# One other hand-written order, in which VectorE makes two early products and GpSimd takes half of e from the first unit on

## The chip, the cores and the metric

The kernel runs on one core of a Trainium2 chip. The time is the device time of one execution in microseconds (us); lower is better. Five instruction streams matter here, each strictly in order: TensorE (PE), VectorE (DVE), ScalarE (ACT), GpSimd (POOL) and SyncE (SP), which only issues DMAs. An execution has a span (first to last instruction in the profile) and a time of its own that is a little longer than the span.

## What is computed

Two layers are fused: a gated recurrence along the sequence, and a highway feed-forward layer on its result. With x and f_logit of shape (4, 6336, 256):

```python
sig = 1.0 / (1.0 + np.exp(-f_logit))
f = lower_bound + (1.0 - lower_bound) * sig        # per channel
for t in range(S):
    h = f[:, t] * h + (1.0 - f[:, t]) * x[:, t]
    y[:, t] = h
H = np.maximum(y @ w_h, 0.0)                       # tokens flattened
T = 1.0 / (1.0 + np.exp(-(y @ w_t + b_t)))
out = T * H + (1.0 - T) * y
```

All inputs and the output are float32 in HBM: 52 MB are read and 26 MB written.

## The kernel before, in words

**Tiles.** Work is cut into 25 units. Units 0 to 23 hold 1024 tokens of one batch entry as 8 blocks of 128 tokens, and unit n continues the recurrence of unit n-4. Unit 24 holds the last 192 tokens of all four batch entries as 8 blocks of 96. The recurrence half of a unit is called a *front*, the feed-forward half a *back*. `CUTS` (L44) cuts some units: unit 0 has three fronts (2, 2 and 4 blocks), units 1 and 2 have two fronts of 4 blocks, and unit 24 has two fronts and two backs of 4 blocks. So there are 30 fronts and 26 backs: fronts 0, 1 and 2 are unit 0, fronts 3 and 4 are unit 1, fronts 5 and 6 are unit 2, and front n is unit n-4 for n from 7 to 27. Back j is unit j up to 23; backs 24 and 25 are the halves of unit 24.

**Steps of a front.** Each step has a letter in the order described below. The channels lie in two halves h of 128.

- L, X (L106, SP): the DMA of f_logit into `lt` and of x into `xt`; 1 MB for a whole unit.
- U (L158, ACT): u = sigmoid(-lt), for all 8 blocks in one instruction.
- P (L164, POOL) or p (L170, DVE): bv = u * xt, two blocks to an instruction, so four for a whole unit. Which products are p and not P stands in the list `EARLY` (L69), which is empty here.
- A (L202, PE): 8 transposes of u into PSUM (uT); F (L209, ACT): f = 1 + ncc*uT, one instruction for each h.
- B (L219, PE): 4 transposes of bv into PSUM (bT); S (L234, DVE): the scan y = f*y + bT, one for each h.

**Steps of a back.** W (L152, DVE) makes the weights `w_sb` once, from w_h and w_t, which Q (L129, SP) loads. G and Z (L249, PE) are the matmuls gp and zp, four of 512 columns for each h; both read the y of both channel halves. T (L255, ACT): t = sigmoid(zp + b_t). D (L260, DVE): d = max(gp, ncc*y). E (L170, DVE) and H (L164, POOL): e = d*t, E the first columns and H the rest. O (L300, L301, PE): the output tokens of 4 blocks in PSUM, from y and e. C (L307, ACT) and V (L307, DVE) copy them to SBUF; V does a share in the last three backs only. R (L313, SP) stores them.

**Who does e.** `shared` (L265) gives the number of columns of e that GpSimd makes: 512 of 1024 for full backs from back 3 on, none for backs 0 to 2, whose e DVE makes in one instruction of 128x2048.

**The port rule.** `gpsimd_mul` (L162) makes each GpSimd product wait for every DVE product (E or p) that stands before it in the order since the last GpSimd product.

**The order.** It is written out by hand: `PLAN` (L353) is a string in which each letter issues the next instance of its step, and every engine executes its instructions in the order of the string. In A, B, Z, G and O the digit behind the letter is the PSUM slot. uT and bT share two small slots, gp, zp and op share three large ones, and a step waits until the one before in its slot has been read. M (L373, PE) is a matmul on a tile of zeros whose result nobody reads; 22 of them lie in the first part of the string. L and X wait for a free buffer of five each (`BUFS`, L78), and SP issues loads and stores from one queue, so that a store that waits for its copy holds back the loads behind it.

In the running part both engines that matter most go round like this, once for a unit: DVE `S D E S D`, ACT `F T C F T C U` in changing order. D works on the unit whose scan was finished just before.

Of the kernel before, what the change touches and what calls it, by code (L numbers as in the profile page):

```python
# [19 lines left out]
def kernel(  # L20
# [19 lines left out]
    P = 128  # L40
    NH = D // P
    NB = 8
# [16 lines left out]
    fronts, backs = [], []  # L59
# [6 lines left out]

    LASTQ = 2

    EARLY = []  # L69

# [40 lines left out]
    def shape(piece):  # L113

        u, j0, j1 = piece
        return units[u][0], j1 - j0
# [38 lines left out]
    def gate(i):  # L155
        np_, nb = shape(fronts[i])
        u = fs[i]["u"] = new("u", [NB, D], FP16)
        pin(nc.scalar.activation(u[:np_, :nb], fs[i]["lt"][:np_, :nb], AF.Sigmoid, scale=-1.0))  # L158
# [13 lines left out]
    def product(i, k, mul):  # L172
        np_, _ = shape(fronts[i])
        if "bv" not in fs[i]:
            fs[i]["bv"] = new("bv", [NB // 2, D, 2], BF16)
        mul(inner(fs[i]["bv"][:np_, k:k + 1])[:, 0], fs[i]["u"][:np_, 2 * k:2 * k + 2],
            fs[i]["xt"][:np_, 2 * k:2 * k + 2])

    def width(piece):
        np_, nb = shape(piece)  # L180
        return np_ * nb
# [81 lines left out]
    SHARE = 512  # L263

    def shared(j):  # L265

        return SHARE if width(backs[j]) == NB * P and j >= 3 else 0

    def e_cols(j, a, e):
        if "e" not in bs[j]:  # L270
# [3 lines left out]
    def e_dve(j):  # L274
        vector_mul(*e_cols(j, 0, width(backs[j]) - shared(j)))

    def e_pool(j):
        gpsimd_mul(*e_cols(j, width(backs[j]) - shared(j), width(backs[j])))
# [37 lines left out]
    def each(pieces, count):  # L316
        return [(i, k) for i, piece in enumerate(pieces) for k in range(count(piece))]

    def halves_of(pieces):
        return each(pieces, lambda p: len(halves(p)))  # L320
# [11 lines left out]
        "U": (lambda i, _: gate(i), each(fronts, lambda p: 1)),  # L332
        "P": (lambda i, k: product(i, k, gpsimd_mul), [p for p in products if p not in EARLY]),
        "p": (lambda i, k: product(i, k, vector_mul), [p for p in products if p in EARLY]),
        "A": (decay_pe, halves_of(fronts)),
# [7 lines left out]
        "D": (d_dve, each(backs, lambda p: NH)),  # L343
        "E": (lambda j, _: e_dve(j), each(backs, lambda p: 1)),
        "H": (lambda j, _: e_pool(j), [(j, 0) for j in range(len(backs)) if shared(j)]),
        "O": (o_pe, groups),
        "C": (lambda j, q: o_copy(j, q, nc.scalar.copy, 0, group(j, q)[2]), [p for p in groups if group(*p)[2]]),
# [3 lines left out]
    }  # L351

    PLAN = (  # L353
        "XLLLXXLXLQQUUMMMMMMMMMMMA0MA1PFFFUFUMB0PSSMMMMB1A0FFPSSPMMMMMB1A0XLLXLXXPFUFSSWWPB1A0G0Z1PFFUPSSDPXL"
        "LXLB0A1G2Z0PUTFFTPPB1SSDUSSEZ1A0G0G2A1DDPFTFFPPZ1A0B1O0O2PSSTFECCUB0Z1B1G0G2SDSDA0Z0TUFTPPPPPPA0G1B1"
        "FXLLLXRRXLXDESA0Z0Z2O1UFTCTB0G0A1O1O2SDPPPFCCB1A0Z1G0O2FTUCB0G1PPPHPSDSEDPA1Z0Z2B0O1FTUCTESA1G0G1B0D"
        "DHPPPPSZ2O0O1FUTCCB1SA0G2Z0B1FDUTPHPPSXXLRLRRRLRXLRRZ1A0G2O0PDTFCEEG1B1A0O2O0UFCCDSG1B0A1Z2Z0SDPHPPP"
        "PFTTA1B0O2O1G0HPSFCCZ2B1A0Z1DUTFTEG0O2PSPLXXRXRRRRDPPHCB1SA0O1G0Z2B1FCUTDEPSG1Z0A0O2FTCPDPPHB1A0Z1G0"
        "O2SFTCDEB0Z1A1G0PLLXRRRRSDPPPUFTO2B0A1Z0G1SHDCFTEO2B0G0Z1A1PPPPCUFTSDHO2B0A1G0Z1SCFTO2B0A1DEPSZ1G0PP"
        "PCUFTDHO2B0A1O0G1SCFCDEZ2B0A1Z0PSTFTPPPG1B1O2A0O0DUCFCSG1Z2A1B0HDELXLLRXRLLRXRRRRRXPSTFPPZ1G0O2B1DTC"  # L360
        "SZ1G2A0O0PHUFTCDEB1A0G2Z1O0PSPFTCDPPHB0G1G2A1Z0UFTSA0B1FDEDSPO1O0Z2B0PPCCTPHSO1A1G0Z2B0UFTCDEPSA1G0Z"
        "2O1PPDB0FTCSA1Z2G0O1PHFUCTDELXRRXXRRLRLXXRRRA1B0G0Z1PSFTO2DCB1A0G1Z0O2PPPHSUFCTDEB1A0Z1G2O0PSDFTCB0A"
        "1Z1G2SFPPPHDO0B1A0G2ETUCFPSO1PZ0CDTB1A0Z1G2SFTUHO0A0B1DFG1EPPPPSO2A0CCZ0DFB1O2Z1B0TCUTSESHPPG0A1Z2G1"
        "DDRRRRRRRRFFTA1B0O2Z0Z1FCFSEHTTG2B1G0O1RSDDCO2SRHCZ0G1STRO2TDDEZ0CTERTG1O2O0DVDVCO2CREVO1CRO0RCVRR"
    )
    assert set(PLAN) <= {*kinds, *"M012"}
    assert all(PLAN.count(k) == len(places) for k, (_, places) in kinds.items())
# [36 lines left out]
```

## Time and profile before

| what | value |
|---|---|
| median of 3 runs | 212.41 us (211.95 to 212.56) |
| profiled execution, its own time | 212.41 us |
| its span | 210.6 us |
| DVE busy | 195.0 us (93%) |
| ACT busy | 193.6 us (92%) |
| PE busy | 191.6 us (91%), mean granted clock 0.989 |
| POOL busy | 160.7 us (76%) |
| DMA | 78.69 MB, 374 GB/s over the span |

An engine's busy time is the union of its instructions' spans. On ACT one instruction's span can reach into the next one's, so the distance from start to start is the better measure of what an instruction costs there. "Idle before" in the groups is the time that the engine had nothing under way, with the instruction or the transfer that ended it.

### The profile page before, as it was taken

How to read it: one execution, taken by the hardware profiler on the slowest of the kernel's cores; microseconds unless marked ns; L12 is line 12 of the kernel's file. 1: busy time of each engine (PE TensorE's matmuls, PEld its weight loads, DVE VectorE, ACT ScalarE, POOL GpSimd, SP SyncE). 2: the span in 40 equal slices, each digit the busy share in tenths (PEclk: the TensorE clock that was granted, in tenths of full speed). 3: DMA queues.
4: the chain of work that ended last, by engine and by line, in shares of the span. 5: the costliest groups of instructions: out<-in, count | busy, mean ns of one | idle time of the engine just before them, and what ended most of it. 6: DMA issues, size and time to landing. Idle time of an engine off the chain costs nothing.

```text
span 210.6 us, 4661 instructions
## 1 busy us (share of the span) xinstructions
PE 191.6 (91%) x1822; PEld 132.3 (63%) x1822; DVE 195.0 (93%) x155; ACT 193.6 (92%) x194; POOL 160.7 (76%) x133
## 2 busy tenths in 40 slices
PE   7759988899889999999999999999999999999970
PEld 2336564586565866767667666658576676855770
DVE  2379999999999999999999999999999999999980
ACT  3687999999999999999999999999999999998750
POOL 4667685797799698978998898898889867866400
PEclk9997999999999999999999999999999999999998
DMA  5999999999999999999999999999999997252465
GB/s 133 416 409 429 422 429 428 428 422 419 422 426 422 416 424 419 429 426 415 425 419 429 426 420 426 423 413 429 417 428 412 365 412 310 100 204 100 195 261 195
DMA packets 17350, 78.69 MB, mean 374 GB/s; under 512 B 2352, under 2 KB 2864, under 8 KB 11952
## 3 DMA queue, kind: packets, MB, share of 16 engines
q1 hardware_dynamic: 16784, 78.39, 90.9%
q8 instruction: 14, 0.23, 0.4%
q10 hardware_dynamic: 544, 0.00, 0.1%
q14 instruction: 8, 0.07, 0.1%
HBM read 52.43 MB, written 25.95 MB: 372 GB/s over the span
## 4 chain that ended last, share of the span: by engine, by line
ACT 45%; PE 35%; issue 10%; DMA 3%; POOL 1%; DVE 1%; SPq 1%; ACTq 1%; POOLq 0%; DVEq 0%
ACT t L255 15%; ACT f L209 11%; ACT u L158 10%; PE zp L249 10%; ACT o L307 9%; PE gp L249 7%; PE op L300 5%; PE op L301 5%; PE uT L202 4%; PE bT L219 4%; DMA xt<-in_x_dram 3%; POOL bv L164 1%; SPq L106 1%; DVE o L307 1%; DVE y L234 1%
## 5 line engine op out<-in xcount | busy, mean ns | idle before, releaser
L164 POOL TENSOR_TENSOR bv<-u,xt 128x512 bf16<-128x512 f16 (+1 forms) x100 | 114.4, 1175 | 29.9 <-DVE e L170 13.4
L234 DVE TENSOR_TENSOR_SCAN y<-f,y,bT 128x1024 bf16<-128x1024 f16 (+3 forms) x56 | 106.4, 1917 | 2.3 <-PE bT L219 2.1
L209 ACT ACTIVATE f<-uT,ncc 128x1024 f16<-128x1024 f16 (+3 forms) x60 | 65.3, 1104 | 2.0 <-PE uT L202 2.0
L255 ACT ACTIVATE t<-zp,bt 128x1024 bf16<-128x1024 f32 (+1 forms) x52 | 63.1, 1238 | 0.3 <-DVE e L170 0.3
L260 DVE SCALAR_TENSOR_TENSOR d<-y,ncc,gp 128x1024 bf16<-128x1024 bf16 (+1 forms) x52 | 62.4, 1209 | 0.3 <-issue 0.2
L249 PEld LDWEIGHTS <-w_sb 128*128 128x128 f16 x400 | 37.8, 98 | 37.4 <-issue 5.6
L307 ACT COPY o<-op 128x1024 f32<-128x1024 f32 (+2 forms) x50 | 54.7, 1142 | 4.1 <-PE op L301 2.1
L158 ACT ACTIVATE u<-lt 128x2048 f16<-128x2048 f32 (+3 forms) x30 | 53.1, 1774 | 4.2 <-DMA lt<-in_f_logit_dram 4.2
L249 PE MATMUL gp<-y,w_sb 128*128 128x512 bf16 (+1 forms) x200 | 51.0, 380 | 0.8 <-ACT o L307 0.2
L249 PE MATMUL zp<-y,w_sb 128*128 128x512 bf16 (+1 forms) x200 | 50.4, 376 | 1.2 <-DVE d L260 0.6
L300 PE MATMUL op<-diag,y 128*128 128x128 f16 (+1 forms) x400 | 49.2, 219 | 1.9 <-ACT t L255 0.7
L164 POOL TENSOR_TENSOR e<-d,t 128x1024 bf16<-128x1024 bf16 x21 | 44.8, 2133 | 7.5 <-DVE e L170 2.6
L301 PE MATMUL op<-ident_b,e 128*128 128x128 bf16 (+1 forms) x400 | 49.2, 219 | 0.0
L301 PEld LDWEIGHTS <-e 128*128 128x128 bf16 (+1 forms) x400 | 44.7, 114 | 5.6 <-issue 3.4
L300 PEld LDWEIGHTS <-y 128*128 128x128 bf16 (+1 forms) x400 | 44.8, 114 | 2.7
L219 PE MATMUL bT<-ident_f,bv 128*128 128x128 f32 (+1 forms) x200 | 31.6, 279 | 4.1 <-DVE y L234 1.6
L202 PE MATMUL uT<-ident_h,u 128*128 128x128 f16 (+1 forms) x400 | 30.9, 220 | 4.0 <-ACT f L209 2.3
L202 PEld LDWEIGHTS <-u 128*128 128x128 f16 (+1 forms) x400 | 26.4, 99 | 11.3 <-issue 5.3
L219 PEld LDWEIGHTS bT<-ident_f,bv 128*128 128x128 f32 (+1 forms) x200 | 22.5, 143 | 11.2 <-POOL bv L164 5.0
L170 DVE TENSOR_TENSOR e<-d,t 128x1024 bf16<-128x1024 bf16 (+2 forms) x26 | 19.1, 741 | 0.1
L234 DVE TENSOR_TENSOR_SCAN y<-f,bT 128x512 bf16<-128x512 f16 (+2 forms) x8 | 10.5, 1339 | 2.8 <-PE bT L219 2.8
L373 PE MATMUL busy<-filler 128*128 128x512 bf16 x22 | 7.2, 468 | 1.2 <-DVE filler L120 1.2
(22 smaller groups left out, 12.8 us busy)
## 6 DMA issues: line engine op xcount, KB each, us to landing
out_dram<-o SPq DMA_DIRECT2D x48, 512.0 KB, 13.5
lt<-in_f_logit_dram SPq DMA_DIRECT2D x21, 1024.0 KB, 14.9
xt<-in_x_dram SPq DMA_DIRECT2D x21, 1024.0 KB, 15.9
lt<-in_f_logit_dram SPq DMA_DIRECT2D x5, 512.0 KB, 7.6
xt<-in_x_dram SPq DMA_DIRECT2D x5, 512.0 KB, 8.2
lt<-in_f_logit_dram SPq DMA_DIRECT2D x2, 384.0 KB, 13.0
xt<-in_x_dram SPq DMA_DIRECT2D x2, 384.0 KB, 11.6
xt<-in_x_dram SPq DMA_DIRECT2D x2, 256.0 KB, 4.5
```

Source lines behind the costliest of these rows:

```text
L158: pin(nc.scalar.activation(u[:np_, :nb], fs[i]["lt"][:np_, :nb], AF.Sigmoid, scale=-1.0))
L164: ins = pin(nc.gpsimd.tensor_mul(out_, a, b))
L202: pin(nc.tensor.transpose(uT[:, j * np_:(j + 1) * np_], fs[i]["u"][:np_, j, h * P:(h + 1) * P], ident_h[:np_, :np_]))
L209: pin(nc.scalar.activation(f[:, :N].rearrange("p (k q j) -> p k q j", q=np_, j=j), fs[i]["uT", h].rearrange("p (k j q) -> p k q j", q=np_, ...
L219: pin(nc.tensor.transpose(t[:, k // r, k % r], fs[i]["bv"][:np_, k, h * P:(h + 1) * P].rearrange("p d j -> p (d j)").bitcast(FP32), ident_ ...
L234: pin(nc.vector.tensor_tensor_scan(y, fs[i]["f", h][:, c:c + w], fs[i]["bT", h][:, c:c + w], 0.0 if prev is None else prev, op0=ALU.mult, ...
L249: pin(nc.tensor.matmul(p[:, a:e], w_sb[:, k, ki, h * P:(h + 1) * P], y_of(j)[:, ki, a:e], start=ki == 0, stop=ki == NH - 1))
L255: pin(nc.scalar.activation(bs[j]["t"][:, m, :width(backs[j])], bs[j]["zp", m], AF.Sigmoid, bias=bt[:, m:m + 1]))
L260: pin(nc.vector.scalar_tensor_tensor(bs[j]["d"][:, m, :width(backs[j])], y_of(j)[:, m], ncc[:, m:m + 1], bs[j]["gp", m], op0=ALU.mult, op1 ...
L300: pin(nc.tensor.matmul(o, y[:, h, cols], diag[:, h], start=True, stop=False))
L301: pin(nc.tensor.matmul(o, bs[j]["e"][:, h, cols], ident_b, start=False, stop=True))
L307: pin(copy(bs[j]["o", q][:np_, a:e], bs[j]["op", q][:np_, a:e]))
```

## The change

`EARLY` names two products: the one of front 0 and the first of front 2 are made on DVE (letter p). `shared` no longer asks for j >= 3, so that GpSimd makes half of e for backs 0 to 2 as well (three more H; E of these backs shrinks to 128x1024). And the whole string `PLAN` is another one. Its letters are the same but for the two p in place of two P, three more H, and 21 M in place of 22. The order differs nearly everywhere: the first loads are L0 L1 X0 X1 L2 X2 and then the weights, S of front 3 stands behind G, G, Z and D, D of back 0, stores stand further ahead among the loads, and the last steps of back 25 (Z, T, T, E) stand further back.

```diff
-    EARLY = []
+    EARLY = [(0, 0), (2, 0)]
...
     def shared(j):
 
-        return SHARE if width(backs[j]) == NB * P and j >= 3 else 0
+        return SHARE if width(backs[j]) == NB * P else 0
...
     PLAN = (
-        "XLLLXXLXLQQUUMMMMMMMMMMMA0MA1PFFFUFUMB0PSSMMMMB1A0FFPSSPMMMMMB1A0XLLXLXXPFUFSSWWPB1A0G0Z1PFFUPSSDPXL"
-        "LXLB0A1G2Z0PUTFFTPPB1SSDUSSEZ1A0G0G2A1DDPFTFFPPZ1A0B1O0O2PSSTFECCUB0Z1B1G0G2SDSDA0Z0TUFTPPPPPPA0G1B1"
+        "LLXXLXQQUUMMMMMMMMMA0pFFMMMMB1PSLXLXLXLSA0MMMMB1UFFpSSWWMMA0PFFUXLXLMMB1PSA0PSUFFUPPG0G1Z2B1DDSZ0STT"
+        "A0B1PPHEFFUPSXXLA0SPFFUO1B0O2LLXXA1PSSPCCFFUPG0G1B0PPPDSSDZ2Z0A1A0TTFFEZ2B1Z1A0TTUFG0G2SDDB1HPPPPHPO"
...
-        "2O1PPDB0FTCSA1Z2G0O1PHFUCTDELXRRXXRRLRLXXRRRA1B0G0Z1PSFTO2DCB1A0G1Z0O2PPPHSUFCTDEB1A0Z1G2O0PSDFTCB0A"
-        "1Z1G2SFPPPHDO0B1A0G2ETUCFPSO1PZ0CDTB1A0Z1G2SFTUHO0A0B1DFG1EPPPPSO2A0CCZ0DFB1O2Z1B0TCUTSESHPPG0A1Z2G1"
-        "DDRRRRRRRRFFTA1B0O2Z0Z1FCFSEHTTG2B1G0O1RSDDCO2SRHCZ0G1STRO2TDDEZ0CTERTG1O2O0DVDVCO2CREVO1CRO0RCVRR"
+        "A0PDPPHCUCFSG2Z1B1Z0A0TFTDEPSPG2O1B0A1G0UCFDPPHSDO2Z1B1A0Z0TFTCPSPG1B0A1EZ0O2FTCUDSG1A1Z0B0RRRRRXRRE"
+        "DHFFO2G1B1TCPSRO0A0O2PCCFDSERG1G0RDSHZ2Z1B1DFTTSZ2G0O1HTTSDDCO2G1EERDO0CDO2CVRO1RCVZ0RCVTRTEO2O1CVRR"
     )
```

The step each letter stands for, with its front or back, follows from counting: the n-th U is the gate of front n, two S and two F belong to a front, two T and two D to a back. The first part of the string before, up to the scan of front 7, gives ACT the order U0 U1 F0 F0 F1 U2 F1 U3 F2 F2 F3 U4 F3 F4 F4 U5 U6 T0 F5 F5 T0 U7 F6 T1 F6 F7 T1 F7 C0 C0 U8, and the changed one U0 U1 F0 F0 U2 F1 F1 F2 F2 U3 U4 F3 F3 U5 T0 T0 F4 F4 U6 F5 F5 U7 C0 C0 F6 F6 U8 T1 T1 F7 F7. On DVE the order before is S0 S0 S1 S1 S2 S2 W W S3 S3 D0 S4 S4 D0 S5 S5 E0 D1 D1 S6 S6 E1 S7, and the changed one p0 S0 S0 p2 S1 S1 W W S2 S2 D0 D0 S3 S3 E0 S4 S4 S5 S5 D1 S6 S6 D1 E1 S7.

More of the change, by code (lines that the diff above doesn't have):

```diff
@@ L353 @@
     PLAN = (
-        "XLLLXXLXLQQUUMMMMMMMMMMMA0MA1PFFFUFUMB0PSSMMMMB1A0FFPSSPMMMMMB1A0XLLXLXXPFUFSSWWPB1A0G0Z1PFFUPSSDPXL"
-        "LXLB0A1G2Z0PUTFFTPPB1SSDUSSEZ1A0G0G2A1DDPFTFFPPZ1A0B1O0O2PSSTFECCUB0Z1B1G0G2SDSDA0Z0TUFTPPPPPPA0G1B1"
-        "FXLLLXRRXLXDESA0Z0Z2O1UFTCTB0G0A1O1O2SDPPPFCCB1A0Z1G0O2FTUCB0G1PPPHPSDSEDPA1Z0Z2B0O1FTUCTESA1G0G1B0D"
-        "DHPPPPSZ2O0O1FUTCCB1SA0G2Z0B1FDUTPHPPSXXLRLRRRLRXLRRZ1A0G2O0PDTFCEEG1B1A0O2O0UFCCDSG1B0A1Z2Z0SDPHPPP"
-        "PFTTA1B0O2O1G0HPSFCCZ2B1A0Z1DUTFTEG0O2PSPLXXRXRRRRDPPHCB1SA0O1G0Z2B1FCUTDEPSG1Z0A0O2FTCPDPPHB1A0Z1G0"
@@ L359 @@
-        "O2SFTCDEB0Z1A1G0PLLXRRRRSDPPPUFTO2B0A1Z0G1SHDCFTEO2B0G0Z1A1PPPPCUFTSDHO2B0A1G0Z1SCFTO2B0A1DEPSZ1G0PP"
-        "PCUFTDHO2B0A1O0G1SCFCDEZ2B0A1Z0PSTFTPPPG1B1O2A0O0DUCFCSG1Z2A1B0HDELXLLRXRLLRXRRRRRXPSTFPPZ1G0O2B1DTC"
-        "SZ1G2A0O0PHUFTCDEB1A0G2Z1O0PSPFTCDPPHB0G1G2A1Z0UFTSA0B1FDEDSPO1O0Z2B0PPCCTPHSO1A1G0Z2B0UFTCDEPSA1G0Z"
-        "2O1PPDB0FTCSA1Z2G0O1PHFUCTDELXRRXXRRLRLXXRRRA1B0G0Z1PSFTO2DCB1A0G1Z0O2PPPHSUFCTDEB1A0Z1G2O0PSDFTCB0A"
-        "1Z1G2SFPPPHDO0B1A0G2ETUCFPSO1PZ0CDTB1A0Z1G2SFTUHO0A0B1DFG1EPPPPSO2A0CCZ0DFB1O2Z1B0TCUTSESHPPG0A1Z2G1"
@@ L364 @@
-        "DDRRRRRRRRFFTA1B0O2Z0Z1FCFSEHTTG2B1G0O1RSDDCO2SRHCZ0G1STRO2TDDEZ0CTERTG1O2O0DVDVCO2CREVO1CRO0RCVRR"
+        "LLXXLXQQUUMMMMMMMMMA0pFFMMMMB1PSLXLXLXLSA0MMMMB1UFFpSSWWMMA0PFFUXLXLMMB1PSA0PSUFFUPPG0G1Z2B1DDSZ0STT"
+        "A0B1PPHEFFUPSXXLA0SPFFUO1B0O2LLXXA1PSSPCCFFUPG0G1B0PPPDSSDZ2Z0A1A0TTFFEZ2B1Z1A0TTUFG0G2SDDB1HPPPPHPO"
+        "1O0B0UCCSSZ2A1G1Z0B0EDTFTPPSPPPA1O2G1O0DHFUCCB1A0G1Z2Z0SFTTA1B0DEPSLLLXXRXRRLXRRRFUPG2O1B1O0A0DPPHCC"
+        "G2FSDZ1Z0A1B0G2EPSTTFUPO1O0B1DPPHCCA0G2Z1SFDZ0A1B0EPSTFTUPG2O1A1B0O0DPPHCCG2Z1FSDA0B1Z0EPRRRRXLLSTFT"
@@ new lines @@
+        "PO2G1B0O0DPUCCESZ1G2A1Z0TFDB0A1G1PHPSDTFUO2B1O0CCPPPHSA0G1Z2Z0B1DFTEPSA0G1O2TPFDPPHB0O0G1A1UCCFSXLRX"
+        "RRLRRRLLRXXDZ2Z0B0A1EPSTTFPO1G2B1A0O0DPPHCUCFSG1Z2Z0B1A0DEPSTTFPG1O2B0O0A1DPPHUCFCSG1Z2DA1B0Z0EPSG1P"
+        "TFTDPPHB1O2O0G1A0UCCSZ2B1Z0FTDEPXRXRRRLRSTPA0O1G2O0B1DPPHFCCSA0G1Z2Z0B1DUFTEPSA0G1O2TPFCO0B0A1G2DPPH"
+        "CSFUDZ1Z0A1B0G2EPSTTFPLLRRXLXRRXRRDPPHO1O0B1A0CCSFUG1Z2Z0A0B1DTTFEPSPG1O2O0B1A0DPPHCCFUSZ2G1A0B1Z0DE"
+        "PSTTFPG1O2O0B1A0DPPHCCFUSG2Z1B0Z0A1RLRRRRXLRXXLLDEPSTFTPG2O1B1O0A0DPPHCUCFSG2Z1B1Z0A0DTTFEPSG2O1B1O0"
```

## The prediction, made before the result was known

> **What bounds the kernel now.** First the page's slices, then the busy time by stages that I cut at DVE's marks: first scan (8.24 us), S of front 7 (32.76), S of front 27 (183.86), end of the last S (198.4), end of the last V (205.4).
>
> ```profile
> PEclk9997999999999999999999999999999999999998
> DMA  5999999999999999999999999999999997252465
> ```
> ```profile
> 8.24:16.34 8.10, 5.38 (x38) 3.36 (x37) 6.41 (x9) 5.48 (x8) 6.20 (x6) 0.90 1.04 413
> 16.34:32.76 16.42, 14.97 (x123) 9.65 (x122) 16.34 (x14) 15.64 (x18) 11.25 (x10) 0.94 1.02 426
> 32.76:183.86 151.10, 145.07 (x1427) 102.27 (x1426) 150.08 (x100) 151.10 (x139) 129.75 (x99) 1.00 0.98 405
> 198.40:205.40 7.00, 5.89 (x80) 4.85 (x77) 6.33 (x12) 4.44 (x8) 0.33 (x1) 1.00 0.74 300
> ```
>
> Columns: stage, length, busy PE, PEld, DVE, ACT, POOL, granted clock, DMA share, GB/s. From 16.3 us on DVE is never without work: 150.08 of 151.10 us in the middle. ACT is as full. From start to start the timeline gives, for one unit, DVE 2 S of 2.255, 2 D of 1.175 and E 0.60, together 7.46 us; ACT 2 F and 2 T of 1.0, 2 C of 0.9 and U of 1.81, together 7.6. ACT is thus 0.13 us a unit slower and lives on a lead: F of front 8 ends 4.3 us before its scan starts, F of front 27 only 2.7. POOL needs 4 x 1.13 + 2.1 = 6.6, PE about 7.0. The DMA engines are full until about 172 us. So little is left to win outside the ramp and the last microseconds; what an order can do is lose DVE time.
>
> The ramp, DVE first, then PE with the granted clock, then POOL:
>
> ```profile
> 8.24 1.26 DVE L234 TENSOR_TENSOR_SCAN y<-f,bT 128x256 bf16<-128x256 f16 x2 [2.77 <-PE bT L219]
> ...
> 12.54 2.45 DVE L234 TENSOR_TENSOR_SCAN y<-f,y,bT 128x512 bf16<-128x512 f16 x2 [1.17 <-PE bT L219]
> 14.91 1.39 DVE L152 SCALAR_TENSOR_TENSOR w_sb<-o,cc 128x512 f16<-128x512 f32 x2
> 16.34 2.33 DVE L234 TENSOR_TENSOR_SCAN y<-f,bT 128x512 bf16<-128x512 f16 x2
> ...
> 32.76 2.27 DVE L234 TENSOR_TENSOR_SCAN y<-f,bT 128x1024 bf16<-128x1024 f16 x1
> ```
> ```profile
> 15.14 1.09 PE L219 MATMUL bT<-ident_f,bv 128*128 128x128 f32 x4 [1.61 <-DVE y L234]
> 16.02 1.06 PE L202 MATMUL uT<-ident_h,u 128*128 128x128 f16 x8
> 16.87 1.69 PE L249 MATMUL gp<-y,w_sb 128*128 128x512 bf16 x4
> 18.40 1.03 PE L249 MATMUL zp<-y,w_sb 128*128 128x512 bf16 x4
> ```
> ```profile
> 14.00:15.00 1.00, 0.00 (x0) 0.00 (x0) 1.00 (x2) 1.00 (x2) 0.29 (x1) 0.89 1.04 424
> 15.00:16.00 1.00, 0.86 (x4) 0.85 (x5) 1.00 (x2) 0.78 (x2) 0.13 (x1) 0.50 1.05 430
> ...
> 18.00:19.00 1.00, 1.00 (x5) 0.42 (x4) 1.00 (x2) 1.00 (x2) 0.45 (x1) 0.90 1.11 459
> ```
> ```profile
> 19.65 2.29 POOL L164 TENSOR_TENSOR bv<-u,xt 128x512 bf16<-128x512 f16 x2 [1.21 <-DMA xt<-in_x_dram]
> 23.31 2.30 POOL L164 TENSOR_TENSOR bv<-u,xt 128x512 bf16<-128x512 f16 x2 [1.37 <-DMA xt<-in_x_dram]
> ```
>
> DVE idles 2.77 us ahead of its first scan and 1.65 more up to 12.54, then hardly. PE finds its clock at half for about 3.3 us after a gap of 1.61: four gp matmuls take 1.53 from start to start, against 0.86 at full clock. The POOL rows give the clock of the DMA: X5 is the transfer up to which 6.0 MB stand in SP's queue, X6 that at 7.5 MB, so 1.5 MB land in 3.66 us, 2.44 us a MB (MB of 2^20 bytes, as the page's KB); at the middle's 422 GB/s it is 2.485. From X6 a landing can be worked out for any load.
>
> **The change, part by part.** Sums are against the profiled execution, 212.41 us with a span of 210.6 and 1.8 around it; the median of the runs is the same 212.41.
>
> *DVE's own work.* Three E of 128x2048 (1.12 from start to start) become 128x1024 (0.60): -1.56. Two products come in. DVE has none in this trace: with e's rate for 512 elements it would be 0.30, with W's row (128x512, one float32 operand, 0.70) 0.70; float32 makes W the nearest, I take 0.65, +1.3 for two. Together -0.3 us of 192. POOL gets three H of 2.1 and loses two P of 1.13: +4.0, beside 30 us of waiting ahead of its bv group; where its products come later, S is what waits, and the walk below has it.
>
> *The ramp, up to S of front 7.* Both orders have by then issued the same S, D, E and W on DVE, so this one start time says what the ramp is worth. Before: 32.76. After, walked by hand: X2 stands at 2.0 MB in both queues and landed at about 9.5 before (its P started at 9.56), so p2 runs 9.5 to 10.15; it stands ahead of S1, which can't use the earlier first scan (about 7.3 in place of 8.24). S1 to 11.4, W to 12.8, S2 to 15.15. The same work, without the products, ended at 16.3 before: 1.15 us won. But then the order has D0 ahead of S3, and B3, for S3, behind G, G, Z on PE. G needs the y just finished, so DVE stands still. If the clock is at half from 14.9 to 18.2 as before, G, G run 15.2 to 18.3, Z to 19.2, B3 to 19.6, and S3 starts at 19.65. Z of the other half ends at 20.5, T0 at 21.5, and from there ACT alone sets the pace: F4, F4, U6, F5, F5, U7, C, C, F6, F6, U8, T1, T1, F7 are 12.8 us, S7 starts at 34.35: **+1.6**. At full clock G, G end at 16.9, T0 at 20.1, S7 at 33.05: +0.3. Nothing earlier is possible: L8 stands at 9.5 MB, lands at 23.31 + 2.0 x 2.46 = 28.2, and U8, T1, T1, F7 behind it are 4.8 us. The early zeros don't decide it: M are 21 in place of 22, and in my walk PE is as sparse from 9 to 15 us and then idle 1.8 us. I take the row that is nearest, half clock.
>
> The Trainium skill speaks for the other end. Its page "TensorE: Matmul & The Clock Gate", section "HAM oscillation — how this bites in real kernels", has the clock drop only after PE idles for longer than about 3.4 us. By that rule 1.8 us would not do it and the sum would be 1.3 us lower; this trace shows the drop after 1.61 us behind sparse work, and the trace decides.
>
> *After S7* one E is still to shrink: **-0.5**.
>
> *The middle.* ACT's lead over DVE is smaller in the new order. Adding start-to-start times along each engine's order from S7, F after its ACT predecessors is late for S by at most 0.6 us in the order before (the trace shows 1.02 us of DVE idle there, 0.4 more) and by up to 1.7 (S of front 25) in the new one. From no loss to 1.1 more; since 0.4 of other idle can hide under it, I take **+0.7**.
>
> *The last microseconds.* From S27 to the last S both have the same DVE work, 14.54 us. Behind it (t0 = 198.4 before) back 25's T stand at 200.20, ahead of the copies, and E25 at 203.01:
>
> ```profile
> 200.20 1.05 ACT L255 ACTIVATE t<-zp,bt 128x384 bf16<-128x384 f32 x2 [0.33 <-DVE e L170]
> ```
> ```profile
> 203.01 0.55 DVE L170 TENSOR_TENSOR e<-d,t 128x768 bf16<-128x768 bf16 x1
> ...
> 204.69 0.69 DVE L307 COPY o<-op 96x512 f32<-96x512 f32 x1 [0.27 <-PE op L301]
> ```
>
> In the new order Z25 stands behind three O on PE and in the slot that C23 and V23 free, and T25 behind C24. Walked from t0: E23 at 1.0, E24 to 2.15, D25 to 3.2; O23 to 2.55 and 3.45, O24 to 4.35; Z25 to 5.0, T25 to 6.0, E25 to 6.55, O25 to 7.5, V25 to 8.2. Before it was 205.38 - 198.4 = 7.0. **+1.2**; nothing, if DVE's queue is late anyway.
>
> Sum: 1.6 - 0.5 + 0.7 + 1.2 = +3.0, 215.4 us.
>
> **The rivals.**
> - *The clock stays full at 15 us.* For it: the zeros are placed otherwise. 1.3 us less: 214.1.
> - *The ramp's loss is all there is to see, and it is none.* Full clock, ACT keeps up, the late T25 hides: 0.3 - 0.5 = -0.2, 212.2: no change. Against it: three orders would have to be kinder than their sums.
> - *The ramp pays* (faster). DVE begins with p0 when X0 lands, at 0.75 MB, about 6.3, and idles no more than the 1.7 us it idled behind its first scan before: 6.3 + 24.5 (8.24 to 32.76) + 0.2 = 31.0, and with E2 -2.3: 210.1 without later losses, about 211 with half of them. It decides at L8: it would have to land by 26.2, in place of 28.2. Against it: X5 and X6 put POOL on this very clock.
> - *Loads come late.* L16 stands at 31.5 MB in place of 27.0, X19 at 43.0 in place of 37.5, because stores stand ahead. They land at 82.9 and 111.5 by the same clock; their users are due at about 84 and 111 to 112. No cover is left: landings 2 us later cost about 2: 217.4. For it: DMA at 9 in all these slices; against it: every other load has 2 us or more.
>
> **How the numbers follow.** Chances: forecast 0.42, full clock 0.20, no change 0.14, faster 0.11, late loads 0.13. A measurement of this kernel can tell about 0.3%, 0.64 us, from no change: faster 0.11, same 0.14, slower 0.75. The range leaves out the faster case and the far part of the late loads: 212.0 to 217.5.
>
> **What would show it.** Right: S of front 7 at 34.3, a DVE gap of 1 us or more ahead of the first D with four gp matmuls at 1.5 us, E1 or S7 waiting for ACT, DVE idle of 1.5 us or more in the middle, and E25 waiting for T25. Wrong: S of front 7 before 32.5; PEclk without its 7; ACT idle behind T0, which breaks the walk's saturation; or POOL as the engine that S waits for in the middle, which I have priced at nothing.

## The result, and the profile after

The changed kernel takes 214.13 us (median of 4 runs, 214.02 to 214.66), the kernel before 212.49 us (4 runs, 211.95 to 212.57): a ratio of 1.0088, 95% interval 1.0064 to 1.0111. It is slower by about 1.6 us; 215.4 was predicted. The profiled execution after took 214.1 us, with a span of 212.3: 1.7 us more than the span before.

First the page's slices after, clock and DMA share.

```profile
PEclk9999699999999999999999999999999999999998
DMA  5999999999999999999999999999999996547085
```

The dip of the clock has gone from the fourth fortieth (15.8 to 21.1 us) to the fifth (21.2 to 26.5 us). Next the stages after, cut at the same marks of DVE as before: first scan (7.48), S of front 3 (17.86), S of front 7 (35.07), S of front 27 (185.54), and from the end of the last S (200.05) to the end of the last V (208.83). Columns as before: busy PE, PEld, DVE, ACT, POOL, clock, DMA share, GB/s.

```profile
7.48:17.86 10.38, 7.72 (x51) 3.97 (x48) 9.33 (x11) 7.33 (x11) 6.34 (x6) 1.00 1.04 416
17.86:35.07 17.21, 13.10 (x113) 9.46 (x112) 14.28 (x13) 16.00 (x19) 14.40 (x13) 0.90 1.02 427
35.07:185.54 150.47, 145.35 (x1414) 102.10 (x1413) 149.80 (x100) 150.12 (x139) 132.52 (x100) 1.00 0.98 398
200.05:208.83 8.78, 6.13 (x85) 4.94 (x82) 6.54 (x12) 5.15 (x8) 0.38 (x1) 1.00 0.73 281
```

By DVE's marks the difference from before is put together so: S of front 7 starts 2.31 us later (35.07 against 32.76); from there to S of front 27 the new order is 0.63 faster (150.47 against 151.10); S27 to the last S is the same (14.51, 14.54); the last copy ends 1.78 later still (8.78 against 7.0); and from the last copy to the end of the span it takes 1.7 less (3.5 against 5.2). Where the ramp's 2.31 arise, DVE's rows show:

```profile
15.47 2.47 DVE L260 SCALAR_TENSOR_TENSOR d<-y,ncc,gp 128x1024 bf16<-128x1024 bf16 x2 [0.47 <-PE gp L249]
...
20.10 0.96 DVE L170 TENSOR_TENSOR e<-d,t 128x1024 bf16<-128x1024 bf16 x1
...
25.64 2.33 DVE L234 TENSOR_TENSOR_SCAN y<-f,bT 128x512 bf16<-128x512 f16 x2 [2.13 <-PE bT L219]
...
33.22 1.40 DVE L170 TENSOR_TENSOR e<-d,t 128x1024 bf16<-128x1024 bf16 x1
35.07 2.29 DVE L234 TENSOR_TENSOR_SCAN y<-f,bT 128x1024 bf16<-128x1024 f16 x1 [0.46 <-PE bT L219]
...
44.08 1.12 DVE L170 TENSOR_TENSOR e<-d,t 128x1024 bf16<-128x1024 bf16 x1
...
173.86 0.69 DVE L170 TENSOR_TENSOR e<-d,t 128x1024 bf16<-128x1024 bf16 x1
```

The gap ahead of the first D, priced at over 1 us, is 0.47. But DVE stands still for 2.13 us ahead of the scan of front 5, and the three E of half the size, E0 to E2, are 0.96, 1.40 and 1.12 us long, where the same instruction later takes 0.69 (at 173.86). PE's rows say who holds up the scan:

```profile
15.06 1.24 PE L249 MATMUL gp<-y,w_sb 128*128 128x512 bf16 x5 [0.58 <-DVE y L234]
...
23.10 0.30 PE L301 MATMUL op<-ident_b,e 128*128 128x128 bf16 x1 [1.21 <-POOL e L164]
...
24.47 1.06 PE L219 MATMUL bT<-ident_f,bv 128*128 128x128 f32 x4
...
34.33 0.63 PE L219 MATMUL bT<-ident_f,bv 128*128 128x128 f32 x4 [0.89 <-ACT f L209]
```

The gp matmuls run at full clock (five take 1.24 us). At 23.10 O of back 0 has waited 1.21 us for GpSimd's half of e, H0, though its first half needs only tokens that DVE made: in the tile e (128 x 2 x 1024) each channel half holds DVE's 512 columns and then GpSimd's, so DVE's two pieces and GpSimd's two interleave, and the matmul waits for both (run 1 below takes the pieces apart, and the wait goes). B5, the bT group at 24.47, stands behind O on PE and runs at half clock (1.06 us for four, 0.63 at full clock). The clock by single microseconds:

```profile
22.00:23.00 1.00, 0.00 (x0) 0.00 (x0) 1.00 (x2) 1.00 (x3) 1.00 (x1) 0.83 1.05 442
...
24.00:25.00 1.00, 1.00 (x10) 1.00 (x8) 0.00 (x0) 1.00 (x2) 1.00 (x2) 0.50 0.98 401
25.00:26.00 1.00, 1.00 (x10) 0.94 (x9) 0.36 (x1) 0.88 (x1) 0.31 (x1) 0.50 0.97 410
26.00:27.00 1.00, 1.00 (x20) 1.00 (x19) 1.00 (x2) 0.22 (x1) 0.10 (x1) 0.97 1.04 442
```

The other late place is ACT's. The chain of waits within 14 to 45 us, from the page's own tracing back (start, length, what):

```profile
14.38 14.81 DMA lt<-in_f_logit_dram
...
29.27 1.87 ACT u L158
...
32.08 1.10 ACT t L255
33.18 0.31 ACT f L209
...
34.07 1.12 ACT f L209
35.19 1.34 ACT t L255 x2
```

It goes through the load L8 to U8 (29.27), the T's of back 1 behind it, F of front 7, and from then on along ACT. The slots of PSUM tie S7 to that too: its bT at 34.33 had to wait for F. ACT's rows have two waits there, 0.90 us of a C for O of back 0 and 0.31 of U8 (the releaser named for U8 had ended 4 us before; the chain names L8's landing):

```profile
24.88 1.00 ACT L307 COPY o<-op 128x1024 f32<-128x1024 f32 x1
26.78 1.01 ACT L307 COPY o<-op 128x1024 f32<-128x1024 f32 x1 [0.90 <-PE op L301]
...
29.27 1.91 ACT L158 ACTIVATE u<-lt 128x2048 f16<-128x2048 f32 x1 [0.31 <-POOL bv L164]
...
35.07 2.14 ACT L255 ACTIVATE t<-zp,bt 128x1024 bf16<-128x1024 f32 x2
```

### The profile page after: what moved, and what is told of

The parts are those of the page before. It is cut to its first block, busy times and chain, and to the rows that moved or that the text cites. A ratio compares the mean times of both kernels' runs of the same rounds, so it can differ in the third digit from the quotient of the medians.

```text
span 212.3 us, 4645 instructions
## 1 busy us (share of the span) xinstructions
PE 192.5 (91%) x1821; PEld 133.0 (63%) x1821; DVE 196.5 (93%) x157; ACT 194.4 (92%) x194; POOL 164.8 (78%) x134
## 4 chain that ended last, share of the span: by engine, by line
PE 43%; ACT 27%; DMA 13%; DVE 9%; issue 4%; POOL 1%; SPq 1%; ACTq 0%; DVEq 0%; POOLq 0%
PE gp L249 11%; DMA lt<-in_f_logit_dram 11%; PE zp L249 9%; ACT f L209 9%; ACT t L255 8%; PE op L300 7%; ACT u L158 7%; PE op L301 7%; PE bT L219 5%; DVE y L234 5%; PE uT L202 5%; ACT o L307 3%; DVE d L260 3%; DMA xt<-in_x_dram 2%; POOL e L164 1%
## 5 line engine op out<-in xcount | busy, mean ns | idle before, releaser
L164 POOL TENSOR_TENSOR bv<-u,xt 128x512 bf16<-128x512 f16 (+1 forms) x98 | 112.0, 1175 | 26.3 <-DVE e L170 9.6
L209 ACT ACTIVATE f<-uT,ncc 128x1024 f16<-128x1024 f16 (+3 forms) x60 | 67.5, 1144 | 0.7 <-PE uT L202 0.7
L255 ACT ACTIVATE t<-zp,bt 128x1024 bf16<-128x1024 f32 (+1 forms) x52 | 61.3, 1279 | 1.3 <-PE zp L249 0.9
L158 ACT ACTIVATE u<-lt 128x2048 f16<-128x2048 f32 (+3 forms) x30 | 54.0, 1801 | 5.4 <-DMA lt<-in_f_logit_dram 4.7
L164 POOL TENSOR_TENSOR e<-d,t 128x1024 bf16<-128x1024 bf16 x24 | 51.6, 2151 | 8.7 <-DVE e L170 7.4
L301 PE MATMUL op<-ident_b,e 128*128 128x128 bf16 (+1 forms) x400 | 50.5, 222 | 2.9 <-DVE e L170 1.7
L300 PE MATMUL op<-diag,y 128*128 128x128 f16 (+1 forms) x400 | 50.6, 221 | 0.7 <-ACT t L255 0.7
L249 PE MATMUL zp<-y,w_sb 128*128 128x512 bf16 (+1 forms) x200 | 49.5, 376 | 1.2 <-DVE y L234 0.8
L170 DVE TENSOR_TENSOR e<-d,t 128x1024 bf16<-128x1024 bf16 (+1 forms) x26 | 18.8, 726 | 0.7 <-ACT t L255 0.5
```

The costliest lines, as they stand in the source:

```text
L164: ins = pin(nc.gpsimd.tensor_mul(out_, a, b))
L209: pin(nc.scalar.activation(f[:, :N].rearrange("p (k q j) -> p k q j", q=np_, j=j), fs[i]["uT", h].rearrange("p (k j q) -> p k q j", q=np_, ...
L249: pin(nc.tensor.matmul(p[:, a:e], w_sb[:, k, ki, h * P:(h + 1) * P], y_of(j)[:, ki, a:e], start=ki == 0, stop=ki == NH - 1))
L255: pin(nc.scalar.activation(bs[j]["t"][:, m, :width(backs[j])], bs[j]["zp", m], AF.Sigmoid, bias=bt[:, m:m + 1]))
L300: pin(nc.tensor.matmul(o, y[:, h, cols], diag[:, h], start=True, stop=False))
L301: pin(nc.tensor.matmul(o, bs[j]["e"][:, h, cols], ident_b, start=False, stop=True))
```

## The experiments

Three ideas stood at the start: the ramp's loss comes from **H0** (O, then B5, at half clock); or from **L8** (U8 stands ahead of T1 and F7 on ACT and waits for its load); and the late T25 is **hidden** because the last stores end later anyway. Against each stood the plain reading that DVE binds and every wait of DVE is lost. Later a fourth was added: that **ACT** binds the changed kernel, and not the kernel before, where it has a lead.

The kernel before took 213.3 to 213.5 us on the chips of these runs; all ratios are to its runs on the same chip. The first scan starts 0.6 to 1.4 us later in their profiles, mostly because the first loads land later, so marks are compared within one profile.

**1. e in two blocks.** The changed kernel, with DVE's and GpSimd's halves of e in separate blocks.

```diff
-            bs[j]["e"] = new("e", [NH, NB * P], BF16)
-        return (bs[j][key][:, :, a:e] for key in "edt")
+            bs[j]["e"] = new("e", [2, NH, 512], BF16)
+        return (bs[j]["e"][:, a // 512, :, :e - a], bs[j]["d"][:, :, a:e], bs[j]["t"][:, :, a:e])
...
-                pin(nc.tensor.matmul(o, bs[j]["e"][:, h, cols], ident_b, start=False, stop=True))
+                pin(nc.tensor.matmul(o, bs[j]["e"][:, c, h, ecols], ident_b, start=False, stop=True))
```

> The changed kernel, with e laid out so that VectorE's half and GpSimd's half are two separate blocks instead of interleaved columns; nothing else differs. Theory 1 (the ramp is lost because O of back 0, though it reads VectorE's half only, waits for GpSimd's H0, and B and S of front 5 stand behind it on PE): the 2.13 us of DVE idle ahead of S of front 5 go, the half clock behind that gap too, S of front 7 comes from 35.07 to 33 to 34, the time from 214.1 to 212.3 to 213.2. Theory 2 (the order itself, D0 ahead of S3 and U8 ahead of T1, holds the ramp): S of front 5 comes sooner, but S of front 7 stays within 0.5 us of 35.07 and the time within 0.5 us of 214.1.

Ratio 1.0090 [1.0055, 1.0124]: no gain. Yet the wait it was made against is gone, as DVE's rows of this kernel show, and its ACT row says what took its place:

```profile
24.70 2.33 DVE L234 TENSOR_TENSOR_SCAN y<-f,bT 128x512 bf16<-128x512 f16 x2 [0.51 <-PE bT L219]
...
34.00 1.39 DVE L170 TENSOR_TENSOR e<-d,t 128x1024 bf16<-128x1024 bf16 x1 [2.19 <-ACT t L255]
```
```profile
30.05 1.91 ACT L158 ACTIVATE u<-lt 128x2048 f16<-128x2048 f32 x1 [1.40 <-POOL bv L164]
```

DVE's 2.13 us shrink to 0.51, and 2.19 us appear further on, ahead of E1, whose T1 stands behind U8 on ACT. (The product that is named as U8's releaser had ended 4 us before; in the changed kernel the chain above names L8's landing for this instruction.) Taken away by itself, H0's wait gives nothing: L8's takes its place. The same layout in the kernel before, `before_blocks`, is worth nothing either:

> The kernel before with e in two blocks, nothing else. It tells whether the layout is worth anything by itself: in the kernel before, O of backs 0 to 2 has no H to wait for and PE's waits hardly reach VectorE, so it stays within 0.4 us of before, ratio 0.998 to 1.002. If O's wait for H cost time in the running part too, it is faster by more.

Ratio 1.0008 [0.9993, 1.0024].

**2. GpSimd's share left out of backs 0 to 2.** `shared` asks for j >= 3 again, and three H are taken from the string.

> The changed kernel, but VectorE makes all of e for backs 0, 1 and 2 as before the change (three H taken out of the order, nothing else moved). Theory 1: the wait for H0 goes here as well, S of front 5 starts by 24.5; VectorE gets 1.6 us of e back, 1.0 of it before S of front 7; S of front 7 at 34 to 35, the time 213.2 to 214.2. Theory 2: nothing is gained at S of front 7 and the time rises by the 1.6 us of e, to 215 to 215.7. If GpSimd's early share were a gain by itself, this run is slower than the changed kernel.

Ratio 1.0112 [1.0077, 1.0147], against 1.0088 with the share: the share gives some 0.5 us in this order, and the intervals overlap. The pages have DVE busy for 197.8 us here and for 196.5 in the changed kernel, so what the share takes off DVE is 1.3 us.

**3. No product on DVE.** `EARLY = []` and P for p in the changed kernel.

> The changed kernel with the two early products on GpSimd again (P in place of p at the same places of the order). Product 0 then takes 1.17 us in place of 0.73 on the path to the first scan; the product of front 2 no longer stands ahead of front 1's scans on VectorE, but both products of front 2 queue on GpSimd. Theory 1 and 2 alike: VectorE has 1.3 us less work, its first scans come 0.4 us later, S of front 2 at 12.3 to 13, and since D0 waits for S of front 2 and PE, the time stays within 0.6 us of 214.1. If the early products are worth something, it is slower by more.

Ratio 1.0087 [1.0059, 1.0115]: the two early products are worth nothing, and cost nothing. The pages, of this kernel and of the changed one:

```profile
PE 191.7 (90%) x1794; PEld 133.3 (63%) x1821; DVE 194.9 (91%) x155; ACT 194.2 (91%) x194; POOL 167.0 (78%) x136
```
```profile
PE 192.5 (91%) x1821; PEld 133.0 (63%) x1821; DVE 196.5 (93%) x157; ACT 194.4 (92%) x194; POOL 164.8 (78%) x134
```

DVE has 1.6 us less to do here, and the time is the same.

**4. T25 early.** Z, T, T and E of back 25 stand ahead of the copies again, as in the order before.

```diff
-        "DHFFO2G1B1TCPSRO0A0O2PCCFDSERG1G0RDSHZ2Z1B1DFTTSZ2G0O1HTTSDDCO2G1EERDO0CDO2CVRO1RCVZ0RCVTRTEO2O1CVRR"
+        "DHFFO2G1B1TCPSRO0A0O2PCCFDSERG1G0RDSHZ2Z1B1DFTTSZ2G0O1HTTSDDCO2EZ0CTERRTG1O2O0DVDVCO2CREVO1CRO0RCVRR"
```

> The changed kernel with the end of the order taken from the kernel before: Z, T and E of back 25 ahead of the copies of backs 23 and 24. Theory A (the last stores are drained by the DMA engines whatever the last copy does): the last copy ends about 1.7 us earlier after the last scan, but the time changes by less than 0.5 us. Theory B (the prediction's: the late T25 costs its 1.2 us): the time falls by 1.0 to 1.7 us, to 212.4 to 213.1.

Ratio 1.0084 [1.0057, 1.0111]. The rows of DVE show T25's lateness, first in the changed kernel, then the last V here:

```profile
206.45 0.56 DVE L170 TENSOR_TENSOR e<-d,t 128x768 bf16<-128x768 bf16 x1 [0.48 <-ACT t L255]
208.14 0.69 DVE L307 COPY o<-op 96x512 f32<-96x512 f32 x1 [1.13 <-PE op L301]
```
```profile
207.69 0.69 DVE L307 COPY o<-op 96x512 f32<-96x512 f32 x1 [0.27 <-PE op L301]
```

From the end of the last S to the end of the last V it now takes 7.65 us in place of 8.78, and the time is the same. DMA by stretches says why; first this kernel, then the kernel before, both from about where their last copy ends:

```profile
208.00:210.00 2.00, 0.00 (x0) 0.00 (x0) 0.38 (x1) 0.52 (x2) 0.00 (x0) 1.00 1.00 339
210.00:213.20 3.20, 0.00 (x0) 0.00 (x0) 0.00 (x0) 0.00 (x0) 0.00 (x0) 0.61 0.47 158
```
```profile
206.00:208.00 2.00, 0.00 (x0) 0.00 (x0) 0.00 (x0) 0.00 (x0) 0.00 (x0) 1.00 0.98 290
208.00:210.60 2.60, 0.00 (x0) 0.00 (x0) 0.00 (x0) 0.00 (x0) 0.00 (x0) 0.76 0.22 77
```

The DMA share is at 1.00 and 0.98 while the engines have almost nothing left to do: stores drain. In the changed kernel it is at 0.80 from 208 to 210 us and there is less queue left behind its last copy. From the end of the last S to the end of the span all three take the same: 12.2 us before, 12.3 after, 12.5 here. T25's lateness is hidden.

**5. U8 behind F7.** In the changed kernel U8 and its first two products are moved behind F7, so that T1 and F7 no longer stand behind the load.

```diff
-        "A0B1PPHEFFUPSXXLA0SPFFUO1B0O2LLXXA1PSSPCCFFUPG0G1B0PPPDSSDZ2Z0A1A0TTFFEZ2B1Z1A0TTUFG0G2SDDB1HPPPPHPO"
+        "A0B1PPHEFFUPSXXLA0SPFFUO1B0O2LLXXA1PSSPCCFFPG0G1B0PDSSDZ2Z0A1A0TTFFUPPEZ2B1Z1A0TTUFG0G2SDDB1HPPPPHPO"
```

> The changed kernel with U of front 8 moved behind T, T of back 1 and F, F of front 7 on ACT (and with it the first two products of front 8 in the order's text; GpSimd's own order is the same). Theory 3 (what holds S of front 7 is ACT's queue: U8 waits for its load, which lands near 29.3 us, and T1, T1, F7 stand behind it): T1 starts near 30.1, when its matmuls are done, F7 ends near 33, S of front 7 starts at 33.2 in place of 35.07. GpSimd then has the products of front 8 later, H1 behind them, so that S of front 8 may wait; the time falls by 0.5 to 1.9 us against the changed kernel's +1.7, ratio to before 1.000 to 1.006. Theory 4 (the ramp's loss is spread and made good nowhere): ratio stays at 1.007 to 1.010.

Ratio 1.0195 [1.0163, 1.0227]: 4.2 us slower than before, against the expectation. H1 still stood behind P of front 8 on GpSimd, and these now waited for the later U8; S of front 8 began 9.2 us behind S of front 7 (6.8 in the changed kernel), and ACT idled 1.3 us between 45 and 60 us, where it does not idle in the changed kernel. The edit had moved one engine's wait to another's queue, so it told nothing of L8. It was mended:

**6. The same with H1 ahead of U8, and e in two blocks.**

```diff
-        "A0B1PPHEFFUPSXXLA0SPFFUO1B0O2LLXXA1PSSPCCFFUPG0G1B0PPPDSSDZ2Z0A1A0TTFFEZ2B1Z1A0TTUFG0G2SDDB1HPPPPHPO"
+        "A0B1PPHEFFUPSXXLA0SPFFUO1B0O2LLXXA1PSSPCCFFPG0G1B0PDSSDZ2Z0A1A0TTFFHUPPEZ2B1Z1A0TTUFG0G2SDDB1PPPPHPO"
```

> The changed kernel with three edits: e in two blocks, U8 behind F7 as in the run before, and H1 ahead of the products of front 8 on GpSimd. Theory 3: neither the wait for H0 nor the wait for U8 is left, S of front 5 near 23.5, S of front 7 at 31.5 to 32.5 in place of 35.07, and the time falls by 2.0 to 3.0 us against the changed kernel: ratio to before 0.994 to 0.999, faster than both. Theory 4: ratio 1.004 or more.

Ratio 1.0051 [1.0032, 1.0069]. Its rows of DVE and of ACT:

```profile
32.88 2.29 DVE L234 TENSOR_TENSOR_SCAN y<-f,bT 128x1024 bf16<-128x1024 f16 x1 [0.24 <-PE bT L219]
36.45 2.47 DVE L260 SCALAR_TENSOR_TENSOR d<-y,ncc,gp 128x1024 bf16<-128x1024 bf16 x2 [1.28 <-PE gp L249]
```
```profile
37.19 1.92 ACT L158 ACTIVATE u<-lt 128x2048 f16<-128x2048 f32 x1 [0.37 <-DMA lt<-in_f_logit_dram]
```

From the first scan to S of front 7 it takes 24.8 us, as long as before (24.5) and 2.8 less than after (27.6). But DVE loses 1.28 right behind it, and U9 waits for L9; at S of front 9 only 0.7 of the 2.8 are left (41.5 us from the first scan, after 42.3). The time is 0.8 us better than the changed kernel's by the ratios, whose intervals just overlap. So DVE's mark at S7, by which the ramp was judged, overstates what the ramp is worth. With T25 early too:

> The run before with the end of the order taken from the kernel before as well (Z, T, E of back 25 early). Theory A (the stores at the end hide the late T25): within 0.4 us of the run before. Theory B: 1.0 us or more faster than it.

Ratio 1.0065 [1.0046, 1.0084], no better: the hidden tail again.

**7. The loads of run 6 in the order before.** X7 X8 L8 L9 X9 in place of X7 L8 X8 X9 L9 on SP.

> u8_behind_f7_blocks_h1 with the loads behind X7 in the order of the kernel before: X7 X8 L8 L9 X9 in place of X7 L8 X8 X9 L9. L9 then stands 1 MB earlier. Theory (what is left of that kernel's loss is ACT's wait for L9 ahead of U9, 0.37 us and a little more): U9 without a wait for its load, 0.3 to 0.6 us faster than that kernel, ratio to the kernel before 1.002 to 1.004. Rival (L8, which now stands 0.5 to 1 MB later, holds up U8, T1 and F7 by as much): no gain, ratio 1.005 or more.

Ratio 1.0046 [1.0029, 1.0063]. U9 no longer waits for its load (it starts at 37.17 behind T without a gap), but this profile's first scan was 0.5 us later as well, and the times can't be told apart: inconclusive.

**8. Two more instructions on ACT, in both kernels.** Identity of the zero tile, 128x512, twice, behind the second F of front 15.

```diff
+    scratch = singles.tile([P, 2, 512], BF16, name="scratch")
+
+    def load_act(k):
+        pin(nc.scalar.activation(scratch[:, k], filler, AF.Identity))
...
+        "K": (lambda i, k: load_act(k), [(0, 0), (0, 1)]),
```

> The kernel before with two extra ACT instructions (Identity of the zero tile, 128x512) behind the second F of front 15; the output is unchanged. By f of 128x512, 0.575 us each, they take 1.1 to 1.2 us of ACT, in a stretch in which F leads its scan by 2 to 4 us. Theory (ACT is what binds the changed kernel from about 42 us on, and in the kernel before a lead covers it): at most 0.5 us here. Rival (DVE binds both kernels in the middle): at most 0.4 us here and in the changed kernel alike.

> The changed kernel with the same two extra ACT instructions behind the second F of front 15. Theory (ACT has lost its lead and binds from about 42 us on): +0.9 to +1.2 us against the changed kernel, ratio to the kernel before about 1.013. Rival (DVE binds, ACT has slack): at most +0.4 us, ratio 1.009 to 1.010.

Kernel before: ratio 1.0050 [1.0027, 1.0072]. Changed kernel: 1.0120 [1.0095, 1.0145], 0.0032 or 0.7 us above its 1.0088, though the intervals overlap. In the traces the pair takes 1.04 us of ACT in each, at 94 us, and DVE is later by 0.99 us in the kernel before (its shift against the trace before grows from 0.88 at 78 us to 1.87 at 116) and by 1.06 in the changed one (from 0.75 at 80 us to 1.81 at 106); at S of front 27 the shifts are 1.81 and 1.86. The theory's contrast fell, and the rival with it: at 94 us a microsecond of ACT is a microsecond of the kernel before too, and ACT's lead is no cushion. No run put a known time on DVE there, so that ACT binds alone is not shown. How it reaches DVE is seen in a PE row of the kernel before, the same matmuls with the pair, and the D behind them:

```profile
94.85 1.03 PE L249 MATMUL gp<-y,w_sb 128*128 128x512 bf16 x4
```
```profile
96.15 1.02 PE L249 MATMUL gp<-y,w_sb 128*128 128x512 bf16 x4 [0.24 <-ACT t L255]
```
```profile
97.27 1.28 DVE L260 SCALAR_TENSOR_TENSOR d<-y,ncc,gp 128x1024 bf16<-128x1024 bf16 x1 [0.21 <-PE gp L249]
```

F, a few microseconds ahead of its scan, is not what comes late. It is T, which frees the large PSUM slot for the next gp; D waits for that, by 0.2 us at a time, which hardly shows as idle.

**9. GpSimd's share alone, on the order before.** Three H, each right ahead of its E; nothing else is moved.

```diff
-        return SHARE if width(backs[j]) == NB * P and j >= 3 else 0
+        return SHARE if width(backs[j]) == NB * P else 0
```

> The order before with GpSimd's share of e in backs 0 to 2 alone: three H, each right ahead of its E, which shrinks to 128x1024; no product on DVE, nothing else moved. Theory (DVE's 1.56 us are a gain wherever the order gives ACT a lead over it, and the loss of the change is the order's): 0 to 1.5 us faster than before, ratio 0.993 to 1.000. Rival (three H of 2.1 us ahead of GpSimd's next products, and O's wait for H, eat it or more): ratio 1.001 or above, with DVE idle on bT or PE's O waiting for GpSimd between 23 and 42 us.

Ratio 1.0062 [1.0039, 1.0085]: 1.3 us slower. DVE was to have 1.56 less to do; by the page it is busy for 196.4 us, 1.4 more than before. E of back 0 in the kernel before, then E and H of back 0 here:

```profile
25.74 1.20 DVE L170 TENSOR_TENSOR e<-d,t 128x2048 bf16<-128x2048 bf16 x1
```
```profile
27.14 2.40 DVE L170 TENSOR_TENSOR e<-d,t 128x1024 bf16<-128x1024 bf16 x1
```
```profile
26.86 2.12 POOL L164 TENSOR_TENSOR e<-d,t 128x1024 bf16<-128x1024 bf16 x1
```

Half of the work takes twice as long: H began first and ended at 28.98, E ended 0.56 us later. E0 to E2 together take 4.29 us from start to start here, 3.49 in the kernel before.

## Why the prediction was right, and where not

The direction held, and the time lay inside the range: slower by 1.6 us where 3.0 were forecast. That the sum came so near is in part luck, since its terms missed in both directions. By DVE's marks, in which it was drawn up, the ramp cost 2.31 (forecast 1.6), the stretch from S7 to S27 won 0.63 (forecast a loss of 0.2, from -0.5 and +0.7), and what the end lost up to the last copy, 1.78 (forecast 1.2), it made good behind it. Of the signs that were named, S7 waited for ACT, through its bT, and E25 for T25; the gap of 1 us ahead of the first D (0.47), gp at half clock and 1.5 us of DVE idle in the middle (0.67) did not come.

**What binds.** The prediction called DVE and ACT both full and gave ACT 0.13 us a unit more, but priced all steps by DVE's marks. Run 8 shows that a microsecond of ACT at 94 us passes whole to the end, in both orders. So the loss has to be read on ACT too. Busy and idle time up to S of front 27 do not tell it (columns again PE, PEld, DVE, ACT, POOL; before, then after):

```profile
0.00:183.86 183.86, 171.35 (x1607) 117.64 (x1608) 174.15 (x128) 176.38 (x171) 150.86 (x127) 0.99 0.97 400
```
```profile
0.00:185.54 185.54, 172.05 (x1595) 118.13 (x1596) 175.45 (x131) 177.00 (x171) 156.20 (x129) 0.99 0.98 394
```

The mark comes 1.68 us later. ACT has 0.62 more busy and 1.06 more idle time up to it, which is 1.68; but DVE's 1.30 and 0.38 are 1.68 as well, and so it is with every engine, because busy and idle time always add up to the mark. What tells more is how much later an engine starts on the same work. ACT's rows before, behind which it has made the same U, F, T and C as behind those of 24.88 and 35.07 above, and below them the last such pair, before and after:

```profile
25.10 0.72 ACT L209 ACTIVATE f<-uT,ncc 128x512 f16<-128x512 f16 x1
...
33.83 1.21 ACT L255 ACTIVATE t<-zp,bt 128x1024 bf16<-128x1024 f32 x1
...
181.06 2.09 ACT L307 COPY o<-op 128x1024 f32<-128x1024 f32 x2
```
```profile
182.71 1.11 ACT L255 ACTIVATE t<-zp,bt 128x1024 bf16<-128x1024 f32 x1
```

At 25 us ACT is still 0.22 us ahead in the changed kernel, at 34 it is 1.24 behind: the 1.46 are the two waits, of C and of U8, with what they cut off from overlapping. The same comparison all along, for both engines (start after less start before, with the same work behind it, DVE's two products aside):

| at, us (before) | ACT later by, us | DVE later by, us |
|---|---|---|
| 34 | 1.24 | 2.31 |
| 60 | 1.26 | 1.85 |
| 100 | 0.98 | 1.09 |
| 150 | 0.74 | 1.52 |
| 181 to 184 | 1.65 | 1.68 |

So most of the loss is there when the ramp ends, at about 35 us, and the middle adds 0.4 by ACT's starts and takes 0.6 off by DVE's. But neither delay stays as it is. The kernel before has waits of its own (DVE 0.44 us at 74.86; a T on ACT at 90.58 that takes 1.42 from start to start in place of 1.0), and while ACT's delay grows by 0.9 between 150 and 181 us, DVE's grows by less than 0.2. The two engines hand waits to each other, through PE and the PSUM slots. That one of them sets the pace all along is not shown; that ACT does at 94 us is.

Nor do the other kernels decide it. ACT's idle time behind 185 us is 9.4 to 9.7 us in all fourteen profiles, whose spans range over 5.7 us; but DVE's is as constant, 5.7 to 6.0. Both say only that nothing behind 185 us makes a delay good.

**Step by step.**
- *The ramp, +1.6: the step that failed.* It put the loss on half clock at the first G, 1.3 us of it. G ran at full clock: its first three matmuls, which do not need the second scan of front 2, had started at 13.37, so PE was not idle 1.8 us ahead of the rest, but 0.58. The loss by DVE's mark was 2.31 instead. The walk at full clock came to +0.3, bounded by L8, U8, T1, T1 and F7. L8 is the wait that it sized wrong: it was to land at 28.2, and U8 starts at 29.27, 1.07 later. From there to the end of F7's first half are the 4.8 us of the walk, but S7 starts another 0.99 later, because its bT waits for the slot that this F reads (34.33), which the walk had not. The third wait, of O of back 0 for H0, the walk had not either; run 1 shows that it gives nothing when it is taken away alone, because U8's wait for L8 grows from 0.31 to 1.40. Run 6, with both taken away, is 0.8 us faster than the changed kernel, and 1.1 slower than the kernel before.
- *DVE's own work, -0.3 in all.* It rose by 1.5 us (busy 195.0 before, 196.5 after). The two products are 0.73 and 0.75 long, the second 0.63 from start to start (0.65 was taken). But E0 to E2, which were to take 0.60 each, took 0.95, 1.40 and 1.04 from start to start, 3.39 together: of the 3.49 before, 0.1 was saved and not 1.56, since all three began beside a GpSimd product. Run 3 shows that 1.6 us less of DVE's work gain nothing in this order; run 9, in the order before, has 1.4 more of it and is 1.3 slower.
- *The middle, +0.7.* Not seen by DVE's marks (0.67 us idle after, 1.02 before), 0.4 by ACT's starts, and wrong in its path: it looked for F late at S of front 25, and what is seen late in run 8 is T for the gp slot.
- *T25, +1.2.* The copy was later by 1.78, more than said; "nothing, if DVE's queue is late anyway" named the escape, but for the wrong queue. It is the stores that hide it, as run 4 shows.
- *The rivals.* Late loads did not come in the middle: no U waits for its load between 45 and 180 us. "The clock stays full" came true in its condition and in its time (214.1), by another path: S7 did not start at 33.05 but at 35.07.

The Trainium skill bears on E's odd times. Its page "SBUF — State Buffer", section "Who interferes with whom", calls the port pair that VectorE and GpSimd share an exclusive lock, for which a VectorE instruction with two SBUF inputs contends with a GpSimd instruction that reads SBUF, and says that the order of issue decides who blocks. The runs agree: E of 2.40 beside H, and in the changed kernel E of 1.40 (33.22 to 34.62) beside two products that end at 34.06, again 0.56 earlier.

**What stays open.** About 1.1 us of the loss are left when the waits for H0 and L8 are gone (run 6), and no run takes them away. That L9's landing costs something there is argued from one wait of 0.37 us, and run 7 could not tell. Whether a microsecond of DVE in the middle would come out at the end, as ACT's does, was not tried. Why DVE has more to do with the share in the order before is shown in rows only for back 0, by E blocked behind H. No run beat the kernel before.

## What to carry to other kernels

When two engines are both full, find out which one binds before pricing anything: put a known microsecond on each and see whether it comes out at the end (here only ACT was tried). Then compare when each engine starts on the same work, not one mark of one engine; a ramp that brought DVE's mark 2.8 us forward was worth 0.8. Busy and idle time up to a mark add up to the mark on every engine and prove nothing. And look in the page whether a saving arrived: E of half the size saved 0.1 us of 1.56 here. When an instruction is moved behind one queue's wait, look at what stands behind its products on the next engine, or the wait only changes its place.

## What was not expected of the hardware

- **E and GpSimd's products exclude each other.** An E that starts while a GpSimd product runs ends 0.54 to 0.56 us behind the product's end: 20.10 to 21.06 (product until 20.52), 33.22 to 34.62 (34.06), and in run 9 27.14 to 29.54 (28.98). The other way, H takes 2.58 us in place of 2.12 when E has started first. The port rule of the kernel guards only GpSimd's products against E, not E against them.
- **The clock fell around gaps of 1.2 to 1.6 us.** In the changed kernel PE idles 1.42 us up to 20.33 and 1.21 up to 23.10, and the clock is at 0.50 from about 22.7 to 26.0. From 11 to 15 us PE is busy about half of the time, with no gap above 0.8 us, and the clock stays at 1.00. What share the gaps and the sparse work around them have in it was not tested. The skill's page "TensorE: Matmul & The Clock Gate", section "HAM oscillation — how this bites in real kernels", gives as its rule that idle gaps of PE be no longer than about 3.4 us; here, as in the trace before, the clock fell around gaps under half of that, and the measurement decides.
